# A tuned attention-and-MLP kernel: 11 of 29 products on zeros taken out, and all steps put in another order

## The chip, the cores and the metric

The kernel runs on one core of a Trainium2 chip. The metric is the device time of one execution in microseconds, the median of several. A profile of one further execution comes with it.

A core has five engines that run side by side, each with its own queue of instructions taken in order: PE (TensorE, matrix products; weight loads are shown as PEld), DVE (VectorE), ACT (ScalarE), POOL (GpSimd) and SP (SyncE, which issues most DMAs here). [...] An engine whose next instruction waits holds up all that stands behind it.

## The reference

Routed attention in 4 batches of 8 heads, 768 positions, 64 columns; each position is assigned to one of 16 centroids, and a query sees only keys of its own centroid. Then a gated MLP over all 3072 rows.

```python
q_assign = np.argmax(np.einsum('bhsd,hcd->bhsc', q_n, c_n), axis=-1)
k_assign = np.argmax(np.einsum('bhsd,hcd->bhsc', k_n, c_n), axis=-1)
mask = q_assign[:, :, :, None] == k_assign[:, :, None, :]
scores = np.where(mask, scale * np.matmul(q, k.transpose(0, 1, 3, 2)), -1000000000.0)
attn = np.exp(scores - max); attn = attn / (sum(attn) + 1e-09)
x = np.matmul(attn, v)          # heads side by side: 3072 x 512
h = x @ w_in                    # 512 x 2048
out = (h * (1.0 / (1.0 + np.exp(-h)))) @ w_out
```

## The kernel before

**Work.** Positions come in 6 tiles of 128 for keys (numbered 0 to 5) and 6 for queries (6 to 11). Heads are taken in pairs, 0 to 3. For each pair q and k are loaded into `nat`, turned so that the 64 columns lie along partitions, and put into `ab` in float16, together with a one-hot code of the centroid below them (rows 64 to 95). A product of 96 rows (L795, `scores`) then gives score and mask at once. ACT takes the exponential from a PSUM bank `M` into `P` (L798, 512 columns each). PE multiplies `P` by the values `vt` (L823, `pv`), DVE divides (L842 reciprocal, L847 product), PE or a DMA turns the result (L880) into `xt`, and `mlp` follows: up-products (L911), tanh on ACT (L921), gate on DVE (L924), down-products (L941), a copy out of PSUM (L187 on ACT, L189 on DVE) and a store.

**How the one-hot codes come about.** The first 8 tiles of each pair of the first batch are treated in one of two ways. Pairs 0 and 1 (`part4`): PE turns float32 (L611, 4 products of 128 columns for one head), ACT or DVE copies them to SBUF (`ev`, into `ot`), PE multiplies them in float32 by the centroids `st32` (L638, the program's 4 products a head, 8 records in the trace); DVE takes the maximum (L443), subtracts it (L446), marks the largest (L453); the scaled float16 copy (`hi`, L622 or L626) and the marks are turned on PE (L657, 8 products a head) and copied into `ab` (1024 columns, "s16"). Pairs 2 and 3 (`part2`): PE turns float32 (L689), ACT or DVE takes a high part straight into `ab` ("hip", L704 or L706), DVE a low part (L709), PE multiplies in float16 (L734 to L736), DVE marks and turns (L460, 32x32 blocks), and four copies put the codes into `ab` ("put"). The other 4 query tiles and the later batches (`part`) split into high and low (L482, L485), turn by a DMA on SP (L543) and multiply on PE (L558); their sums are made by DVE (L421).

**What sets the order.** No order of work stands in the loops. `build` makes a list of 1883 steps with what each comes after; the compressed list `PLAN` gives each buffer a slot, then the order of the steps, with the engine of each that has a choice. The last loop of the kernel unpacks it and issues the steps one by one, so each engine's queue is the plan's order restricted to that engine. A negative number in the plan is no step: it issues so many products on `zeros` (L1061, 128x256) into a bank that is free then; nothing reads them. A step's name is written here as batch.pair.head.first tile: for a0.1.0 (attention) batch.head.first query tile.

**The steps that the prediction follows.** Centroids: "cturn" turns them in float32 (L333) for `st32`, "cturn2" in float16 (L337, 2 products); "cp" are the copies into place, "cplace" three copies (L344 to L346). "lo" of p0.0.0.8 and p0.1.0.8 are the low parts of the four later query tiles of pairs 0 and 1, each followed by its transposition on SP.

Of the kernel before, what the change touches and what calls it, by code (L numbers as in the profile page):

```python
# [25 lines left out]
    "nl*;ZinTM2%>eCo(6r*rH4*cCch|zkgYh;i+&y*Q%k@LL9aXF)n5PGgXENwdh6IzH?n=^(Z$jp-Nj7i7=B~*m@--`Hb~XA;?SG2h1K)q%E9C80$m"
    "Zbv9SwSZcf8u+_jWXvXSlQc-hM^As0esb>b{-d%kQwA>qd0QL`KN$WSniK+6Z;bJ2@s6-CWbvVY4Q87nGawaI$@$fXSLfo8j_Yobf==_$JAF%V^Z"
    "4+be=L23;R3=L0rx-Dky_b-8(xW;_`(@0Vm(>AqK@&75@m+*A{#s!o2hmT3J-w-qwMM40<8(O#2eycV!K=QDN5-MNr?-w1c|n|#!c#+$o3wvq&lm"
    "qK3E4w#kQ&(6^QWu2Q}0XxI>NUZf#z^l;#JJ;vc0>@T-zxNc!&T)MfGHdgjx)Nhgmn2)+9h=2L<6$?_^%h|h*#R$>0{G*81<-!Dl|E=PI%NEzTve"
    "2$dS{W(>~X|i6|(mU+m(c@-(6pYO!ZK11dYetHAhS&rP=Bh@_ZO$o)a;(QSYnz@77Saa;2Im(VMtAtyQF%isLi8pYHiET6Gd_{6|cNM{8%u?tr^r"  # L30
    "0lTw~jeIx1+{)v(70YjWqHh$mtB%+cCwl7pyxodslzabZb&Ys_k5=mFemgezL*A^Qy<^a>A>!TDeM;C~8}KT~{RnitC%WEn*X{S#8uD_^t?>c-)R"
    "6ZraR2lPc&AA8%Od2>57?22y(Z}O`@K^-`d#AxPYj3cb<yu6$HbA(Tc^*<VfRe}|M|+f?+?G{gJ{Nut?#367_fN|`A>BW|KC~Y^XgQ{`!4d^v(s<"
    "Cb)5fvJB93fhV7l*cMaP6L}MVD?P0r4$6I@}Cj0E_qu*KjR}Gq5Px|f5G;`v*tJT}xyBF_NM{7WS8(}e~qBu@XuDW|KWU?mC)IE1qstU@<+xPrV1"
    "9UvpGPTfgCYTI!oQ9^l`<zT@8}3s8ZDgM3cN(J)KxU{7b)YW10u!MLw1%wE6k0$_s0VGK8N3LyU^dh@x#>7BLp$gKKfp`$w@16eCMXDVU=q9!Tj5"
    "7|6}G`-m;zHF2W*GU@Ca;y9?%n7K?iscvcWXy1iPRc&zz2a05hQ@?1mk1_g=s`fX-mfK6EF%1}oqWerd=C9mLK8zd?5Sl)ldLIhp~P;X~aU%>+%M"
    "h~5?Lh5in6<ulri;3Mph<!|iI<vX-H`UNb6hoCpiQ(Q3C9MT{U?UnK|b{}*<?14|<C#{kGoakXV0*z@mfw!=S!+cl($DuFugItOU=6s5N1}WHopl"
    "`s>unJzsH~rCpCcXkrSLO_%FE{!K45fdB{D%D~{e!W8fdSaVv?p2@6ogzbioUm@5IjsfE98gAX^)06a1<87SQrGwp#XD^X|K_jAsyc28QIY6@(=v"
    "U_<0yf{{{2}oP|Sr9^)6$%a9Mggp+U%u0meM-{ZQ%=sSvUbR2pL7MpkXIja@t^#6sv3*W*LxCVbKUl^MUx3P1>8dwYK6i>=;#Rf#6HQciW{a0iuT"
    "+!MTBjAT1<bWQqm$B~@JJ=6FdkDe9^gW8^MgN73@D+TcnnHgESkFU>(*7E~gkFcD^q*D^z;e|X+W(--lvCI~ID>sd`G~ziH3%&RYoHB04P~Jtlz}"
    "+-o_QtF$Ixfcw$KhLKs?-}zp(s|{Uki0I))a9Z=n=a(jLH5Pz&b4E#_50KY^+g&`;6%umCE;3(yU!F;+tRgIz;y-H*P-XeX$xXE0u!zRH>-h0n07"  # L40
    "Llx}iP!oG0e1Ri6qm!V7p2JvOXaQAew?vnq&#7)Im-X&YkN(n%YgoiRTG1|s|Hsg-3xi;=VoY^Hv8QXG3)E-slgd5pa;l9|`C2)Fmeg6moXPT^>I"
    "nB=@AErTuzSmAj6I9y=8$<9O6we;JrVNJ9*;I;PHlKj`^b0$>>=7`<s);ZqSIgiJP!rvdj$HZjxo0ml;^q6t2U_a(e8`xU>)_9kIa1&ZAO1%Xn;K"
    "oro)4b4b}eY9T|HOHma7OFF|j3OSOS{A1Kdh=futnOI1hE;q*0uVK9Tfe&}%3MsyH-g*^iO8eIm@@~ju2JAM6B7tv=p2M445VI=HSeL{P{2<-l_T"
    "(Pb5hi7JkH<W*9U*>#+y#jh-w}m%gwdxbP3O}sG9;tgOFI1<vZkP6(@q*ZepdI!P^t}zE72B#K^t}xOU=w|tVT*Et_Tyah1XN^RCDly&-i57-Z*;"
    "fLC+#H+gtE-t##&lqw}I`9&qRMj55OK6Lwg+jtT;r+!$IuwIy10;;`++UXYRE`xdOkaZoyGv;1=3|vD@fa#%3u#Xzx|5YtLvO!#=J$Kn~2NJpt-5"
    "))3lb*GGS6`~uIKtr(_Vg}E1%bJ(9V=L?tv`*>zm`no8F(M!yEReKH{V6Dz%bU)fvF#z|tW+M6;{H8qPx(@C~vh#;(7+MN=yfcY8zbbEF4rA}r{!"
    "r&B?WWKbPS8FHr&LE(D^<_vFAQ^;|0g%Ptoo-th9Xc77AiN<D~w%*^Eyx9n$A!9Yrsd$X@o99i^`ACSbl<Ys=?@UkN|(f$IN>borgY!R)a+F!&&A"
    "hp#jasUZ;G<?#A5e=qG3poq~qYFf@ZNY5#-IieoRvehj_AJH3bwgHP!zsXC#&L%&l_q4QOL(f#l=jDQ1h4Guyl=nSVh;38;CXa&=_E{?vM*y(%>$"
    "6%Moei@RX3|wbDDd=?OegHQWPqgD<0=xqKpg*L-O6Ckz9fDX$)4kyg+=L8xNy_skDz~9Ebcg290){{vSjD|=p|8oOs)LXP4(WWBswTi{<{d_tD@W"
    "yL_*S(7U53s_7eFP*tek-(a8%bYz7(AWmEjxOv$ZFzZwC4m41yK(_e3|M)6u~YVa{Xn8_ZPQgkvxndco_kMs-em4Wr;VJOG&#SFjy+z@Lf>xWl_m"  # L50
    ")>(^v9xmvex&MQ35j!h-m_5lya2+8wzGv<v`rn8AjD3NYMBhUPz)9r|LHRbi8Ad|^#uuUk;Rn@1olmeud955!EW#M*t#^RGh>cC?*UDWu#Xaw!W8"
    "q)83u~40$}{=h{%QIz@AEG9IPEWO9|YhX+M852(5u|LDSdZ!cA--ho2mnfMcN;tAv6{)s}`g6VKX0Nub`jNw-4g58$diHz+C0E@)A1<7OSQy#;`v"
    "|*Q>Uw=D|9hiS%#4-U=OQuRx!qFBM*bZqOCF!&C5+;vIg}IYoPw>b~j*c6P`C8x_B3L-=0#zz5<w<sj{cAPC>_EI;}x{Ki-lv@Yb-m}<206?-RI5"
    "A6jVpa<lFp0HZyoZ=o*X!nLjkeBD}rf-kliFPtP0<EDF41x9du`gN?<}vSQ#V&Rm#S#3XZyK}@6of)B6#7ADs03Z0E%b-N@D>b*Y1%&+0J)(Zw1="
    "@U5T?U;D55>$59>kbC`iN}jE;a$;Z1lOrof}xTX-7s@CSSz-tn-$OK4Yy`A`(fz;)I>Qhs1wX~+j<X+HyxW0ympg(t9&aF3%9kDUOCFjf1&9|gHs"
    "&k3Dla2c+^RXC~dM&`Yvm_VO~Q}iXFv+0`y`LPSYBe0FJWHbe4GPa%e4)|SXCtTMV05{-y5@icog?TT?M_f}CEk^$=^qkH-c$Bs6kuv^~-W{!``S"
    "hRH_a^hVq94=uGrA1@5gm<IXU-TjE7$x=-(HwU`xA|6?`daaY`Nkc`+&ZwX}?Q5llGMB_vyP7y99^YIK?UL;>_74<=G|JpN`BstuqZx!=EJ>-%b0"
    "BzTdd!FZ3Fmg$u9&zNP=3>NvUw9^gI~_06RG;`$nB26~XbLpmF|cP;ATCHat=a#K01bu#B+#_~Wq+@e1(I)SmT;27=WFcCW+{rO=A?LQ#14soup!"
    "?Tw#J_%}Kmtsx^d`){PWM<9>=q4yl|KIvXR*iz&*rgP2^uLczhBb;g+BM)8?6vSK+)&M-ueNfHdp@App`8oOgcd>zQ8cokw{<R{ceGB%3PLLF!iq"
    "KKJV5)7@)6BJUm83FIpIsyVzdJLvl2TCa~7+H!2;E2+W%4)?sD&P*mc;m&*)F*nsw;ss!hrr#y*4G^mjs!)At<uIr!ywSg-q`U#Q;EzfkoJ{SiF@"  # L60
    "&9UFmyP#QN1NKSS0$X91&RMR%sCue83O_(e`l`TB*t=nea**qv;obkh{#&uA8lYN0|4r3g#(dcI;HdJ7>(8T?v~TS7Kw{X>*f!-RWK&Io3##Xg&B"
    "gu*s&d_L$~El0XervyW0ygHr(Iroq1b{7*ymJV6?-}pb=E0{xnCvvDy!B(S$tfU>;Gh|1?@BFS@;L4FjkfM#bCc`A>;4B4dn=o#y+6B=KkdFoKk("
    "{UCYr9$-nS8eGxPn4q~6y{xKe=eOSI=ehl^y7z%H~FgT)mj!uDU%&)Gxh<#ZxfWE650<jQeEDjwD<29dkUtwNL#U^XtpuB@kupa8eRpmci)85kl0"
    "aCc`dG7TI_NNdJBVi*P(m9WAhG{Tec?IPaV~Q_m2#sJqEYLf^YY<}2IP^W342_|QVgW|+%nFPz;{L5@uYi^CG0cOPAwfB-Tt_RSH5LEp4CN2J0y|"
    "*|6o*~Vl>1IZU&6nW(AE&<nh&8H_8jF4b{n)A%+;834y_Brxo)QR7b=B)PIv7eEK)2oJ_6mXGXOe6clx%VvtTx?l@ICLs`|)UdSKU64WQiv)<I8*"
# [1032 lines left out]
```

## Time and profile before

| | us |
|---|---|
| three runs | 300.21, 300.11, 300.46 |
| median | 300.21 |
| the profiled execution, whole | 299.89 |
| the profiled execution, span from first to last instruction | 298.1 |
| its last product's end, from the start of the span | 294.97 |
| products on zeros | 29 |

The profiled execution is 1.8 us longer than its span, and 0.32 us shorter than the median. Times in the profile are counted from the span's start. A PE product's record lasts longer than the time until the next can begin, because products are pipelined: how fast they follow each other is read from the chain (the view that goes back from the last instruction to what released it, which gives each piece only the time that it adds), not from their durations.

### The profile page before, as it was taken

To read this page: it belongs to the slowest core of one execution; us is meant where nothing else is said; L and a number is where in the kernel's file an instruction comes from. 1 tells how busy PE (TensorE), PEld (TensorE's weight loads), DVE (VectorE), ACT (ScalarE), POOL (GpSimd) and SP (SyncE) were. 2 spreads that over 40 slices of the span, in tenths; PEclk is the share of its full clock that TensorE was granted. 3 is DMA by queue.
4 is the path that set the end of the run, shared out by engine and by line. 5 is a ranking of instruction groups with operands and counts; after the bars stand their busy time and mean duration, and the time that the engine had idled before them with its cause. 6 is when DMAs were issued, how large, how long until landed. Compare 5 with 4: busy or idle time off the path is not lost.

```text
span 298.1 us, 7899 instructions
## 1 busy us (share of the span) xinstructions
...
## 2 busy tenths in 40 slices
...
GB/s 221 209 304 239 247 264 294 298 231 208 270 248 196 286 256 204 114 213 228 225 158 104 104 244 153 131 93 31 28 26 70 30 3 62 35 109 0 2 50 161
DMA packets 81798, 47.32 MB, mean 159 GB/s; under 512 B 59104, under 2 KB 76768, under 8 KB 81760
## 3 DMA queue, kind: packets, MB, share of 16 engines
...
q14 instruction: 14, 0.11, 0.1%
q10 hardware_dynamic: 144, 0.03, 0.1%
...
## 4 chain that ended last, share of the span: by engine, by line
PE 93%; DVE 3%; POOL 1%; DMA 1%; issue 0%; SPq 0%
PE M L911 28%; PE M L941 28%; PE M L795 19%; PE M L823 11%; PE M L558 2%; PE M L638 1%; PE M L611 1%; DMA nat<-in_k_dram 1%; PE M L1061 1%; PE M L657 1%; PE M L880 1%; POOL vt L189 0%; DVE lo L709 0%; POOL hl L482 0%; DVE hl L485 0%
## 5 line engine op out<-in xcount | busy, mean ns | idle before, releaser
L798 ACT ACTIVATE P<-M 128x512 f16<-128x512 f32 x288 | 153.5, 633 | 12.9 <-PE M L795 12.5
L924 DVE SCALAR_TENSOR_TENSOR gq<-tn,M 128x384 f16<-128x384 f32 (+1 forms) x120 | 65.7, 574 | 49.1 <-ACT tn L921 47.0
L911 PE MATMUL M<-xt,win_s 128*128 128x384 f16 (+1 forms) x576 | 95.9, 308 | 0.0
L941 PE MATMUL M<-wout_s,gq 128*128 128x512 f16 (+1 forms) x400 | 93.3, 370 | 0.0
L795 PE MATMUL M<-ab 96*128 96x256 f16 (+1 forms) x432 | 89.5, 307 | 0.3 <-DVE M L421 0.2
L921 ACT ACTIVATE tn<-M 128x384 f32<-128x384 f32 (+1 forms) x120 | 59.6, 522 | 28.0 <-PE M L911 25.1
L911 PEld LDWEIGHTS <-win_s 128*128 128x128 f16 x576 | 55.0, 97 | 29.4
L189 POOL COPY ab<-ohT 32x384 f16<-32x384 f16 (+2 forms) x65 | 35.2, 543 | 99.0 <-PE M L795 34.7
L941 PEld LDWEIGHTS <-gq 128*128 128x128 f16 x400 | 37.2, 97 | 35.5
L823 PEld LDWEIGHTS <-P 128*128 128x128 f16 x1152 | 45.7, 97 | 9.7 <-issue 0.4
L823 PE MATMUL M<-vt,P 128*128 128x65 f16 x1152 | 49.0, 193 | 0.2 <-DVE oh L453 0.2
L795 PEld LDWEIGHTS <-ab 96*128 96x128 f16 x432 | 37.8, 97 | 17.5 <-issue 1.4
L187 ACT COPY ot<-M 128x512 f32<-128x512 f32 (+1 forms) x18 | 10.4, 583 | 22.0 <-PE M L941 18.1
L485 DVE SCALAR_TENSOR_TENSOR hl<-nat,hl 128x768 f16<-128x768 f32 (+1 forms) x28 | 26.1, 931 | 0.2
L421 DVE TENSOR_REDUCE M<-M 128x192 f32<-128x384 f32 (+1 forms) x28 | 15.2, 544 | 8.5 <-PE M L558 4.8
L460 DVE STREAM_TRANSPOSE ohT<-oh 128x384 f16<-128x384 f16 (+2 forms) x30 | 16.9, 563 | 1.5 <-ACT ab L187 0.7
L189 POOL CAST vt<-nv 128x384 f16<-128x384 f32 x20 | 12.5, 639 | 18.9 <-DMA nv<-in_v_dram 18.5
L189 DVE COPY ot<-M 128x512 f32<-128x512 f32 (+1 forms) x11 | 7.0, 647 | 10.7 <-PE M L941 10.7
L482 POOL TENSOR_SCALAR hl<-nat 128x768 f16<-128x768 f32 (+1 forms) x16 | 12.4, 778 | 5.3 <-DMA nat<-in_q_dram 3.2
L853 DVE TENSOR_TENSOR xn<-M,rz 128x384 f16<-128x384 f32 x24 | 13.2, 553 | 0.7
L558 PEld LDWEIGHTS <-ab 128*128 128x128 f16 x320 | 11.8, 96 | 2.7 <-issue 0.2
L443 DVE TENSOR_REDUCE mx<-M 128x12 f32<-128x192 f32 (+2 forms) x33 | 11.4, 346 | 2.2 <-PE M L638 1.6
...
## 6 DMA issues: line engine op xcount, KB each, us to landing
...
```

The costliest lines, as they stand in the source:

```text
L189: eng(en).tensor_copy(out, in_)
L421: e.nc.vector.tensor_reduce(out=bank(dst)[:, at : at + HC * n].rearrange("p (n c) -> p n c", c=HC), in_=bank(src)[:, 0 : 32 * n].rearrange ...
L460: e.nc.vector.transpose(T(ohT)[:, 0:n, :].rearrange("p n c -> p (n c)"), T(oh)[:, 0:n, :].rearrange("p n c -> p (n c)"))
L485: e.nc.vector.scalar_tensor_tensor(out=dl(), in0=src(), scalar=QS, in1=dh(), op0=ALU.mult, op1=ALU.subtract)
L558: e.nc.tensor.matmul(bank(Lb)[:, 32 * i : 32 * i + 32], a, st, start=True, stop=True)
L795: e.nc.tensor.matmul(bank(sb)[:, at : at + 128 * (c - a)], ab[0:96, kt[m], :], q, start=True, stop=True)
L798: e.nc.scalar.activation(out=T(P)[:, 0:n], in_=bank(sb)[:, 0:n], func=AF.Exp, bias=0.0, scale=ESC)
L823: e.nc.tensor.matmul(bank(O)[:, at : at + D + 1], T(P)[:, c : c + 128], T(vb)[:, VW * m : VW * m + D + 1], start=(m == 0), stop=(m == NJ - ...
L911: e.nc.tensor.matmul(bank(bk)[:, c0 : c0 + n], e.win_s[:, r, ts(fb, 128)], T(X)[:, r, 128 * j0 : 128 * j1], start=(r == 0), stop=(r == NR ...
L921: e.nc.scalar.activation(out=T(tn)[:, 0 : n * per], in_=bank(bk)[:, 0 : n * per], func=AF.Tanh, bias=0.0, scale=1.0)
L924: e.nc.vector.scalar_tensor_tensor(out=gq(f0 // 4)[:, f0 % 4 : f0 % 4 + per, 0:n], in0=T(tn)[:, 0 : n * per].rearrange("p (f c) -> p f c", ...
L941: e.nc.tensor.matmul(bank(bk)[:, 0 : c1 - c0], gq(quarter)[:, fc % 4, ts(t, 128)], e.wout_s[:, fc, c0:c1], start=(fc == 0), stop=(fc == NF ...
```

## The change

Only `PLAN` is another one. No function changes, and the same 1883 steps are done on the same data.

```diff
 PLAN = (
-    "c-mE&2mDXf8^`Z=|Mn&sAuA&zv`A%U?^#A!nOWIHGD6A7%1S9JLXi<d8D&?LO?GyY7613=-1EKqd%fO$o-^*f=RW6oo^yZSe2(7<IF949D$BKfPR"
...
+    "c-mc=2mFrJ`^WERe;2;Xj%05kWM=QZDY9oO5~4_m%<SyFS11W7D<dgnL`HU*MfUi;Kj%KrQ~!Ux-hHk!?sK2}oa?&I`9Ap^zvFQn@H#%nF_vq4oP"
...
 )
```

Unpacked, the two plans differ in three ways.

- **Products on zeros.** Before: 11, then 5, 2, 2, 3, 2, 3 and 1 (29 in all). After: 11, then 1, 1, 2, 1 and 2 (18).
- **Engines.** 118 steps have another engine. Among the early ones: the copy of a value tile pair (cast of `vt`, cv0.0, first head) from POOL to ACT; the high part of p0.1.0.8 from POOL to DVE; one "hip" of pair 3 from ACT to DVE; the float16 copies (`hi`) of p0.0.0.0 and p0.1.1.0 from ACT to POOL, that of p0.1.0.0 from POOL to ACT; the weights' cast cin1 no longer among DVE's first 60 steps. By counts over the program: ACT 461 to 467 steps, POOL 122 to 119, SP 149 to 146, DVE 461 in both.
- **Order.** Nearly every engine's order. The beginnings, one line a step, PE left before and right after ("zeros 5" are five products on zeros):

```
PE before                     PE after
zeros 11                      zeros 11
turn f32 p0.0.0.0  (L611)     turn f32 p0.0.0.0
zeros 5                       zeros 1
cturn2  (L337)                cturn   (L333)
cturn   (L333)                turn f32 p0.0.1.0
zeros 2                       zeros 1
turn f32 p0.0.1.0             cturn2
centroids p0.0.0.0 (L638)     centroids p0.0.0.0
zeros 2                       centroids p0.0.1.0
centroids p0.0.1.0            turn f32 p0.1.1.0
turn f32 p0.1.1.0             turn f32 p0.1.0.0
turn f32 p0.1.0.0             turn codes p0.0.0.0
turn codes p0.0.0.0 (L657)    centroids p0.1.1.0
centroids p0.1.1.0            centroids p0.1.0.0
turn codes p0.0.1.0           scores a0.0.0 (two banks)
centroids p0.1.0.0            centroids p0.0.0.8 (L558)
turn f32 p0.2.0.0  (L689)     turn codes p0.0.1.0
scores a0.0.0                 zeros 2
centroids p0.0.0.8 (L558)     turn f32 p0.2.0.0
scores a0.0.0                 turn codes p0.1.1.0 (both heads)
scores a0.1.0                 scores a0.1.0
scores a0.0.0                 turn f32 p0.2.1.0
turn f32 p0.2.1.0             scores a0.1.0
turn codes p0.1.1.0 (both)    centroids p0.1.0.8 (L558)
scores a0.1.0 (two banks)     scores a0.3.0
zeros 3                       scores a0.1.0
```

```
DVE after, from its 7th step: cp2.0, lo p0.0.0.8, max p0.0.0.0, cp1.2, below, mark p0.0.0.0,
  clear, max p0.0.1.0, below, cplace, hi p0.1.0.8, lo p0.1.0.8, mark p0.0.1.0, max p0.1.1.0,
  below, sum p0.0.0.8, mark p0.1.1.0, max p0.0.0.8
DVE before, from its 8th:     cp2.1, lo p0.0.0.8, max p0.0.0.0, below, mark, max p0.0.1.0, below,
  mark, lo p0.1.0.8, cplace, max p0.1.1.0, below, sum p0.0.0.8, mark p0.1.1.0, max p0.0.0.8
ACT after:  ev p0.0.0.0, ev p0.0.1.0, cp2.1, hi p0.1.0.0, cp0.2, ev p0.1.1.0, cast cv0.0,
  ev p0.1.0.0, s16 p0.0.0.0, exp, s16 p0.0.1.0, hip p0.2.0.0, exp, exp, hip p0.2.1.0, exp, exp
ACT before: ev p0.0.0.0, hi p0.0.0.0, cp2.0, cp0.2, ev p0.0.1.0, cp1.2, hi p0.1.1.0, ev p0.1.1.0,
  ev p0.1.0.0, s16 p0.0.0.0, s16 p0.0.1.0, hip p0.2.0.0, exp, exp, exp, exp, hip p0.2.1.0, exp
SP after, loads by pair: q0, k0 head 0, k0 head 1, later q0, k1, q1, v0, later q1, q2,
  turn p0.0.0.8, k2, q3, later q2, turn p0.1.0.8
SP before:  q0, k0 head 0, later q0, k0 head 1, k1, q1, later q1, q2, k2,
  turn p0.0.0.8, v0, later q3, turn p0.1.0.8
```

From the middle of the first batch on, the same steps stand in both plans a few places apart; the first up-product (L911) is PE's step 111 before and 112 after, and the last nine steps are down-products of the last unit in both.

More of the change, by code (lines that the diff above doesn't have):

```diff
@@ L26 @@
[L26 to L65, printed above, removed]
@@ new lines @@
+    "ZOg>~}(_*OdK~eW=&8gs{ET1)T6dvb?5m5d3B=cg&EfcSj2M@fh1N@6}s8#_~k!9Q&+edwcBLJdxUf9l`HJ@w{W&f(E~xo6q+4I0@$Mj+4U7GT@{"
+    "%UlMd;%$EeQebjj=`^?-^VW+@OHtl*>$ce{}u`8xA5~xo!v-Qy5?<CoE(wD|z#nP5+>k?^CFe~e>LA?1!w-m6e>Bo+<^VK|)%{;wk<$Y%MnxDH4@"
+    "%%S|nkX|9wTF0LkpH@)Mf2Y{vo`LU=*_9@*bX&OXcDbKQ{(4-K~svh`{_0BcGo>%R>&PcVEZRgP6df(H#KgQ-SdFmM~_*DK*R_1Pqg(lzui;Eu7+"
+    "d1!Ds5jBf5L%ez#-%!(-;?voj3)K``PKUe+aGW)fq*-)H^}@ozFDnCC*~$)NdHGfZK2-pAZLc85Y{J)=xdeNU3@p&2AnmT$z;C(ihgV?8hIcgbd!"
+    "j`6NIGoz3hDT(@M^KPx4W7^!gYgb*r)mvhzNfG%v?Qbfx`#$4q$!2WF%re33SI~N=`noF<WB1Jcl7M+r(2f`49qt!+&Fn+wUwu_PePXFgio|UovI"
```

61 lines of the change are left out of this document (48 added, 13 removed).

## The prediction

> **What bounds the kernel now.** I read the page's chain first, then the windows, then the chain piece by piece.
>
> ```profile
> PE 93%; DVE 3%; POOL 1%; DMA 1%; issue 0%; SPq 0%
> ```
>
> The chain is PE for 93% of the span. What is not PE lies at one place, as the windows show (columns: stretch, length, then busy time of PE, PEld, DVE, ACT and POOL).
>
> ```profile
> 1.00:4.00 3.00, 2.72 (x12) 1.71 (x13) 1.73 (x9) 1.00 (x1) 1.28 (x5) 1.00 0.59 177
> 4.00:7.10 3.10, 3.10 (x15) 2.15 (x15) 0.99 (x5) 1.47 (x4) 1.49 (x13) 1.00 0.97 318
> 16.30:29.00 12.70, 12.00 (x182) 9.69 (x181) 12.20 (x29) 12.70 (x27) 9.62 (x19) 1.00 1.04 268
> 40.00:295.00 255.00, 254.97 (x2568) 162.88 (x2566) 177.58 (x399) 195.63 (x396) 52.36 (x78) 1.00 0.61 145
> ```
>
> From 40 us to 295 us PE is busy for 254.97 of 255.00 us: an order can win nothing there, it can only lose. From 16.3 to 29 us ACT has no pause and DVE hardly one; PE is the one that waits. So the change is decided before about 35 us. The chain in order of time (start, length, what) says the same:
>
> ```profile
> 1.24 2.44 DMA nat<-in_k_dram
> 3.68 0.14 issue
> 3.81 1.09 PE M L611 x4
> 4.90 1.07 PE M L1061 x5
> 5.97 0.35 PE M L337 x2
> 6.32 0.35 PE M L333
> 6.67 0.43 PE M L1061 x2
> 7.10 0.53 PE M L611 x4
> 7.63 0.81 PE M L638 x8
> 8.44 0.22 PE M L1061 x2
> 8.66 0.81 PE M L638 x8
> 9.47 0.91 PE M L611 x8
> ...
> 16.29 0.10 POOL ab L189
> ...
> 28.47 0.50 DVE oh L453 x2
> ```
>
> The chain starts with a load, is PE from 3.81 to 16.29 us, goes through POOL and DVE until 28.97, and from there on is PE to the end but for the last copy. Two things are to be seen. First, five products on zeros cost 1.07 us (0.214 each) at 4.90, and two cost 0.22 (0.11 each) at 8.44: the same product at half and at full speed, with the step near 7.2 us (the four transposes cost 1.09 us at 3.81, eight 0.91 at 9.47). The page's granted clock reads full in all these windows, so the halving is read from these rows. Second, 1.07 + 0.43 + 0.22 = 1.72 us of zeros stand on the chain before 16 us.
>
> **The change, part by part.** *Zeros before the first scores.* 5 + 2 + 2 become 1 + 1. At the rows' prices 1.72 us go and 2 x 0.214 = 0.43 stay: 1.29 us, if PE found all its inputs ready. It won't. The work that moves forward also runs longer at half speed, and the second head's transposes now need their load sooner. PE after, by those rows: transposes until 4.90; one zero, 5.11; the centroids' float32 turn, 0.35, 5.46 (its DVE input is ready, below); the second head's four transposes at half speed, 4 x 0.214 = 0.86. Their load moves one place forward on SP; it can land anywhere from 4.7 us (the 2.44 us of the row at 1.24, plus an issue) to 6.0 us (where the load ahead of it landed before, POOL's row below); I take 5.5 us, nearest to the landings around it. So 6.4 us; one zero, 6.6; cturn2 0.35, 7.0; the first head's centroid products 0.81, 7.8, partly before the clock's step; the second head's, 8.6, against 8.66 + 0.81 = 9.47. **PE is about 0.85 us ahead at 9.5 us**, 0.4 to 1.2 by the landing's two ends.
>
> *What DVE makes of it.* What follows needs DVE's marks. DVE rows of before, with one of POOL:
>
> ```profile
> 4.47 0.25 DVE L321 TENSOR_SCALAR cn<-tn,ci 128x64 f32<-128x64 f32 x1
> 7.52 0.69 DVE L485 SCALAR_TENSOR_TENSOR hl<-nat,hl 128x512 f16<-128x512 f32 x1
> 8.48 0.29 DVE L443 TENSOR_REDUCE mx<-M 128x8 f32<-128x128 f32 x1 [0.26 <-PE M L638]
> 8.80 0.30 DVE L446 TENSOR_TENSOR M<-M,mx 128x128 f32<-128x128 f32 x1
> 9.13 0.35 DVE L453 TENSOR_SCALAR gq<-M 128x96 f16<-128x96 f32 x2
> 13.06 0.42 DVE L443 TENSOR_REDUCE mx<-M 128x16 f32<-128x256 f32 x1 [1.33 <-PE M L638]
> 13.52 0.43 DVE L446 TENSOR_TENSOR M<-M,mx 128x256 f32<-128x256 f32 x1
> 14.02 0.43 DVE L421 TENSOR_REDUCE M<-M 128x128 f32<-128x256 f32 x1
> 14.36 0.48 DVE L453 TENSOR_SCALAR gq<-M 128x192 f16<-128x192 f32 x2
> 6.03 0.62 POOL L482 TENSOR_SCALAR hl<-nat 128x512 f16<-128x512 f32 x1 [1.61 <-DMA nat<-in_q_dram]
> ```
>
> Before, DVE idled 1.33 us ahead of 13.06, waiting for pair 1's centroid products. After, it has no such pause, but more to do first. The later queries' load goes back one place on SP (one issue, 0.47), so POOL's high part is done at 6.5 + 0.62 = 7.1, DVE's low part at 7.9, and the first maximum begins at about 7.95 instead of 8.48. Then, in the new order and with 0.03 between instructions (less an overlap like that from 14.02 to 14.36, 0.09, ahead of some): maximum 0.32, cp1.2 0.42, subtraction 0.33, marks 0.36, a clear 0.15 (no dearer than the copy of 0.21 at 11.04), maximum 0.33, subtraction 0.33, cplace 0.72, high part of p0.1.0.8, low part 0.62, marks 0.38, maximum 0.45, subtraction 0.47, sum 0.35. (cp1.2 took 0.42 us on ACT; cplace is three copies, the first of them the row at 11.04, with gaps of 0.03.)
>
> ```profile
> 8.15 0.42 ACT L187 COPY st<-M 64x64 f16<-64x64 f16 x2
> 11.04 0.21 DVE L344 COPY stk<-M 64x128 f16<-64x128 f16 x1
> 24.00 0.69 DVE L706 TENSOR_SCALAR ab<-M 128x512 f16<-128x512 f32 x1
> 25.93 0.94 DVE L189 CAST win_s<-gq 128x1024 f16<-128x1024 f32 x1
> ```
>
> The high part is not seen on DVE from SBUF: the same shape from PSUM took 0.69, half of the 1024-column cast is 0.47; I take 0.6. The sum is 5.83 us, so pair 1's marks begin at 13.78 instead of 14.36: **0.58 us earlier**. The rest of PE's 0.85 is lost to DVE's longer row.
>
> *From there to the end of DVE's stretch.* DVE is full (12.20 of 12.70), so its load counts. In comes one "hip", 0.69; out goes cin1, 0.94, to a later time, and the windows show DVE with room after 40 us (177.58 of 255). One put leaves and one comes. That is 0.25 us less, and 0.58 + 0.25 = **0.83 us** in all, if ACT follows. If cin1 should cost its 0.94 all the same, the "hip" alone stands against the 0.58, and nothing is won (the second rival).
>
> *Zeros after the first scores.* 3 + 2 + 3 + 1 become 2 + 1 + 2. I cost that at nothing:
>
> ```profile
> 16.33 0.49 PE L1061 MATMUL M<-zeros 128*128 128x256 f16 x3
> ```
>
> The first of them stand where the chain has left PE (from 16.29), so what hides them is a wait; with the wait gone they would cost 0.11 each, 4 fewer giving 0.44.
>
> *ACT.* Its rows:
>
> ```profile
> 13.53 0.60 ACT L704 ACTIVATE ab<-M 128x512 f16<-128x512 f32 x1 [0.33 <-PE M L689]
> 14.03 2.06 ACT L798 ACTIVATE P<-M 128x512 f16<-128x512 f32 x4
> ```
>
> Exponentials follow each other every 0.49 us: four in 2.06, of which the last is some 0.60 by itself, (2.06 - 0.60) / 3. After, the first can begin near 12.3 (the first head's codes are turned on PE from 9.5, right behind DVE's marks; ACT is free for their copy at 10.7, behind two copies for pair 1 and the cast; then come two banks of scores), but with the second s16 behind it, which waits for marks at 12.5 on DVE and then eight turns on PE: 13.2. From there ACT has no pause but one near 15 us, where it waits 0.3 for pair 1's scores behind DVE's marks. The cast that comes to ACT costs about 0.5 between two copies before 10.7. One "hip" less gives 0.49 back later. These cancel to within 0.3 us, so ACT by itself is even; that DVE's 0.83 shows in the end rests on DVE being the one that the chain passes through, not ACT.
>
> **Sum:** 299.89 - 0.83 = 299.06 for an execution like the profiled one; the median of the runs lies 0.32 above it: **299.4 us**. Its own range, by the landing's ends and 0.3 for ACT, is 298.9 to 299.8.
>
> **The rivals.**
>
> *All waits shrink.* The plan puts zeros where a pause is expected, and it has fewer. If the nine zeros' places in the first 31 us close up (0.44) and the 16.3 to 29 us stretch loses its PE idle time (12.70 - 12.00 = 0.70, modelled ends making this a lower count), 0.44 + 0.70 come on top: 299.4 - 1.1 = 298.3. Against it: ACT is full in that stretch and its exponentials are the same number.
>
> *The exponentials keep the pace.* ACT is busy 12.70 of 12.70 us. If it, not DVE, holds PE, only its own row counts, and that is even: 300.2.
>
> *The clock's step comes later.* With seven fewer zeros PE idles near 5.5 us, in the stretch that before was full (3.10 of 3.10) just ahead of the step. If the step then slips, the two heads' centroid products and the eight transposes (0.81 + 0.81 + 0.91 = 2.53 us) can take up to twice as long; pair 1's maximum on DVE waits for all of them, less the 0.85 us that PE had gained, 1.7 us: 299.4 + 1.7 = 301.1. It decides if PE's busy share there falls to that of the first 4 us, 2.72 of 3.00 busy by modelled ends, which did not bring the step. For it: the change takes away just what kept PE busy. Against: PE still has transposes and turns there. [...]
>
> *A transposition on SP starves the exponentials: slower.* PE's 25th step is now the centroid product of p0.1.0.8, before three of the scores that ACT wants next. It needs that tile's DMA transposition.
>
> ```profile
> 11.15 1.24 SPq L543 DMA_TRANSPOSE ab<-hl  x1
> ab<-hl SPq DMA_TRANSPOSE x28, 5.1
> ```
>
> DVE's low part ends at about 12.1 now (7.95 plus the terms up to it, 4.19), so the issue is 1 us later than 11.15, and the median landing is 5.1 us after issue: 17.2, while PE reaches that step at about 16. ACT would then lose some 1.2 us; one "hip" less offsets 0.49: 300.2 + 0.7 = 300.9. It decides if it lands after about 16.5. Before, PE asked for it only after 18 us.
>
> **How the numbers follow.** Forecast 0.40; all waits shrink 0.16; the exponentials' pace 0.18; late step 0.12; starved 0.14. A measurement of this kernel can tell about 0.2%, 0.6 us: faster means below 299.6. Of the forecast's own range 0.28 lies below it and 0.12 above; with 0.16 that is 0.44 faster. Within: 0.12 + 0.18 = 0.30. Slower: 0.12 + 0.14 = 0.26. The range reaches from 298.2 to 301.3.
>
> **What would show it.** The chain after should have L638 twice in a row, ending near 8.6; DVE's L453 of 192 columns at 13.8; no pause of DVE ahead of L443 near 13; the first 512-column exponential near 12.3. A granted pair of zeros that still takes 0.21 after 7.2 us would show the late step; an ACT pause near 17 us behind L558 the starving. PE idle after 40 us would make all of this wrong, since nothing here counts on it.

## The result, and the profile after

| | before | after |
|---|---|---|
| median of four runs, us | 300.16 (300.04 to 300.46) | 303.45 (302.73 to 303.72) |
| ratio | | 1.0104 (95% interval 1.0085 to 1.0123) |
| the profiled execution, whole, us | 299.89 | 302.73 |
| its span, us | 298.1 | 300.9 |

The change made the kernel 3.3 us slower; 299.4 had been forecast, at most 301.3. Some executions here are slower as a whole: of the 75 of the kernel before beside the experiments, nine took 307.65 to 308.39 us and the others 299.19 to 302.45; here and below ratios leave such ones out, and medians don't. First the page's chain of the changed kernel:

```profile
PE 82%; DVE 6%; DMA 3%; ACT 2%; issue 2%; POOL 2%; SPq 1%; DVEq 0%; ACTq 0%; POOLq 0%
```

It was PE for 93%. The windows of the changed kernel (stretch, length, busy time of PE, PEld, DVE, ACT, POOL, then clock and DMA) say where PE was lost:

```profile
4.00:7.10 3.10, 3.10 (x17) 2.41 (x16) 1.12 (x6) 1.42 (x4) 0.47 (x1) 1.00 0.79 249
16.30:29.00 12.70, 11.81 (x171) 9.20 (x169) 11.81 (x32) 12.06 (x26) 8.78 (x17) 1.00 1.18 256
30.00:40.00 10.00, 8.98 (x154) 7.45 (x152) 9.41 (x28) 9.63 (x21) 6.92 (x11) 1.00 0.88 247
40.00:295.00 255.00, 254.17 (x2569) 162.67 (x2568) 174.89 (x397) 198.20 (x402) 51.84 (x80) 1.00 0.60 143
13.50:41.00 27.50, 25.57 (x405) 20.87 (x404) 25.80 (x72) 26.49 (x53) 17.89 (x31) 1.00 1.05 256
```

Two stretches of before that were not shown yet:

```profile
30.00:40.00 10.00, 10.00 (x181) 8.61 (x178) 8.93 (x33) 10.00 (x21) 9.19 (x16) 1.00 0.89 257
13.50:41.00 27.50, 26.78 (x432) 22.64 (x431) 25.64 (x73) 27.47 (x57) 21.02 (x38) 1.00 0.99 251
```

Three things are to be seen. From 30 to 40 us PE is busy 8.98 us instead of 10.00. From 40 to 295 us it has 254.17 where it had 254.97: 0.8 us are lost where, before, nothing was. And ACT, which had no pause from 13.5 to 41 us (27.47 of 27.50), now stands still for 1.0 us there.

The same from the starts of the products: what passes from one start to the next beyond the price of the product at full clock (0.109 us for 256 columns, of which one record lasts 0.27, and so on), zeros counted as lost, adds up as follows. PE is ahead by 0.4 us until 30 us, and then loses three times.

| lost by PE, us, up to | 15 us | 30 us | 40 us | 45 us | the end |
|---|---|---|---|---|---|
| before | 5.89 | 9.00 | 9.91 | 10.00 | 10.38 |
| after | 5.41 | 8.56 | 11.08 | 11.68 | 13.00 |

The early steps came as forecast, or sooner. From the timelines of PE, DVE and ACT of the changed kernel:

```profile
6.70 2.00 PE L638 MATMUL M<-st,ot 128*128 128x32 f32 x16
13.16 0.48 DVE L453 TENSOR_SCALAR gq<-M 128x192 f16<-128x192 f32 x2
12.47 0.60 ACT L798 ACTIVATE P<-M 128x512 f16<-128x512 f32 x1 [0.71 <-PE M L795]
13.14 1.01 ACT L187 COPY ab<-M 96x1024 f16<-96x1024 f16 x1
14.04 0.60 ACT L704 ACTIVATE ab<-M 128x512 f16<-128x512 f32 x1
14.53 1.08 ACT L798 ACTIVATE P<-M 128x512 f16<-128x512 f32 x2
```

The two heads' centroid products end at 8.70, and pair 1's marks begin at 13.16, 1.2 us earlier than before. But look at ACT: the first exponential at 12.47 only changed places with a copy and a "hip"; the unbroken row begins at 14.53, where before it began at 14.03. The eighth exponential starts at 17.96 us, against 17.85. Then ACT runs dry, as its timeline after and then before shows:

```profile
16.96 2.09 ACT L798 ACTIVATE P<-M 128x512 f16<-128x512 f32 x4
19.69 1.61 ACT L798 ACTIVATE P<-M 128x512 f16<-128x512 f32 x3 [0.64 <-PE M L795]
```

```profile
16.89 3.61 ACT L798 ACTIVATE P<-M 128x512 f16<-128x512 f32 x7
```

Why it does stands in the chain of the changed kernel:

```profile
13.74 5.10 DMA nat<-in_k_dram
18.84 0.04 issue
18.89 0.55 PE M L689 x3
19.43 0.24 PE M L795 x2
19.69 4.06 ACT P L798 x8
...
31.93 0.87 DVE vt L189
...
34.39 0.30 DVE oh L453
34.69 0.04 issue
34.74 0.82 PE M L795 x6
...
42.40 0.81 DVE hl L485
43.21 0.55 issue
43.76 0.56 DVE M L421
44.33 0.04 issue
44.37 0.60 PE M L911 x4
...
148.07 1.38 DVE hl L485
149.45 0.48 DVE gq L924
149.97 0.81 PE M L911 x4
...
193.73 3.15 DMA ab<-ohT
...
197.01 0.58 DVE ohT L460
197.58 0.03 issue
197.62 0.25 DVE ab L189
197.87 0.03 issue
197.90 0.56 DVE gq L924
198.46 0.04 issue
198.50 0.81 PE M L911 x4
```

Read from above: PE's float32 turn of p0.3.1.0 (L689) waits until the last load of k lands at 18.84, with the scores that ACT wants behind it. At 34 us a PSUM bank is held until DVE has made the marks of p0.3.0.8, behind a cast of 0.87 us that has come from POOL. At 44.37 and 149.97 an up-product waits for a bank that DVE frees late, behind a long low part (L485). At 198.5 it waits for a gate, queued behind a transposition of codes (L460) that waits for a copy by DMA. And the first up-product starts at 41.89 us where it started at 39.83, since the last exponential of the first query tiles, which it needs from all eight heads, starts at 38.10 instead of 35.54.

### The profile page after: what moved, and what is told of

It reads as the page before. It is cut to its first block, busy times and chain, and to the rows that moved or that the text cites. A ratio compares the mean times of both kernels' runs of the same rounds, so it can differ in the third digit from the quotient of the medians.

```text
span 300.9 us, 7860 instructions
## 1 busy us (share of the span) xinstructions
PE 293.5 (98%) x3069; PEld 194.5 (65%) x3069; DVE 208.9 (69%) x502; ACT 232.5 (77%) x469; POOL 74.4 (25%) x135
## 4 chain that ended last, share of the span: by engine, by line
PE 82%; DVE 6%; DMA 3%; ACT 2%; issue 2%; POOL 2%; SPq 1%; DVEq 0%; ACTq 0%; POOLq 0%
PE M L941 27%; PE M L911 25%; PE M L795 18%; PE M L823 10%; PE M L558 2%; DMA nat<-in_k_dram 2%; ACT P L798 2%; DVE hl L485 1%; POOL ab L189 1%; DMA ab<-ohT 1%; DVE gq L924 1%; DVE ab L189 1%; DMA tn<-in_centroids_dram 1%; SPq L410 1%; DVE ohT L460 1%
## 5 line engine op out<-in xcount | busy, mean ns | idle before, releaser
L798 ACT ACTIVATE P<-M 128x512 f16<-128x512 f32 x288 | 151.9, 629 | 15.3 <-PE M L795 13.4
L911 PE MATMUL M<-xt,win_s 128*128 128x384 f16 (+1 forms) x576 | 94.6, 308 | 0.8 <-DVE gq L924 0.6
L941 PE MATMUL M<-wout_s,gq 128*128 128x512 f16 (+2 forms) x400 | 93.7, 370 | 0.0
L911 PEld LDWEIGHTS <-win_s 128*128 128x128 f16 x576 | 55.4, 97 | 30.4 <-issue 1.6
L189 POOL COPY ab<-ohT 32x384 f16<-32x384 f16 (+2 forms) x62 | 33.8, 545 | 70.7 <-DVE ohT L460 25.0
L795 PEld LDWEIGHTS <-ab 96*128 96x128 f16 x432 | 38.1, 97 | 18.8 <-issue 3.9
L187 ACT COPY ot<-M 128x512 f32<-128x512 f32 (+2 forms) x21 | 11.9, 571 | 22.0 <-PE M L941 18.3
L485 DVE SCALAR_TENSOR_TENSOR hl<-nat,hl 128x768 f16<-128x768 f32 (+1 forms) x28 | 27.4, 985 | 2.0 <-POOL hl L482 1.5
L482 POOL TENSOR_SCALAR hl<-nat 128x768 f16<-128x768 f32 (+1 forms) x20 | 16.3, 818 | 25.2 <-DMA nat<-in_k_dram 12.7
L460 DVE STREAM_TRANSPOSE ohT<-oh 128x384 f16<-128x384 f16 (+2 forms) x30 | 16.7, 560 | 6.6 <-DMA ab<-ohT 5.7
L189 POOL CAST vt<-nv 128x384 f16<-128x384 f32 x17 | 8.7, 514 | 29.5 <-DMA nv<-in_v_dram 29.0
L842 DVE RECIPROCAL rz<-M 128x6 f32<-128x6 f32 (+1 forms) x36 | 6.5, 182 | 13.5 <-PE M L823 13.0
L558 PEld LDWEIGHTS <-ab 128*128 128x128 f16 x320 | 11.5, 96 | 3.0 <-DMA ab<-hl 0.3
L453 DVE TENSOR_SCALAR oh<-M 128x96 f16<-128x96 f32 (+3 forms) x56 | 12.1, 255 | 0.7
```

The costliest lines, as they stand in the source:

```text
L189: eng(en).tensor_copy(out, in_)
L460: e.nc.vector.transpose(T(ohT)[:, 0:n, :].rearrange("p n c -> p (n c)"), T(oh)[:, 0:n, :].rearrange("p n c -> p (n c)"))
L482: e.nc.gpsimd.tensor_scalar(out=dh(), in0=src(), scalar1=QS, scalar2=1.0, op0=ALU.mult, op1=ALU.mult)
L485: e.nc.vector.scalar_tensor_tensor(out=dl(), in0=src(), scalar=QS, in1=dh(), op0=ALU.mult, op1=ALU.subtract)
L558: e.nc.tensor.matmul(bank(Lb)[:, 32 * i : 32 * i + 32], a, st, start=True, stop=True)
L795: e.nc.tensor.matmul(bank(sb)[:, at : at + 128 * (c - a)], ab[0:96, kt[m], :], q, start=True, stop=True)
```

## The experiments

All are timed beside the kernel before on the same chip, whose medians were 300.2 to 300.5 us. Diffs show the unpacked plan.

### The zeros alone, and the zeros put back

e1_before_few_zeros is the kernel before, with the changed kernel's zeros at the start:

```diff
-PE: turn p0.0.0.0, zeros 5, cturn2, cturn, zeros 2, turn p0.0.1.0, centroids, zeros 2, centroids
+PE: turn p0.0.0.0, zeros 1, cturn2, cturn, zeros 1, turn p0.0.1.0, centroids, centroids
```

> The kernel before, with the early products on zeros as in the change: 5 become 1, the first 2 become 1, the second 2 go; nothing else differs. If the new order of the steps made the loss (A), this stays within 0.5 us of before: 299.7 to 300.3 us, since DVE and ACT pace the stretch from 16 to 29 us. If the removed zeros made it (B: the clock's step slips), L638 runs slower at 7 to 8 us and the time rises by 1 to 3 us, to 301.2 or more. If each zero on the chain had counted (C), 1.29 us go: 298.9 us.

Ratio 1.0036 (1.0004 to 1.0069), some 1.1 us slower: outside A's range, far from C, and at the lower end of B's. But B's late step is not in its profile, where it comes at 6.99 us (7.16 before). PE has lost 9.04 us by 30 us there, as before (9.00): taking out zeros won nothing, since what PE gains at first it waits off again by 15 us, for loads (0.7 us ahead of its float32 turns, 0.2 before) and for DVE. This profile loses its time later, 1.2 us in three pauses at 52 to 77 us, two of them behind casts of weights on DVE that had waited for their loads. Whether the missing zeros have a part in that is not shown. The runs in the ratio spread from 299.6 to 303.1 us, and three of them had a mean granted clock of 0.993, which none of the 75 runs of the kernel before beside these experiments had (0.998 at least).

e13_after_zeros_back is the reverse, and e12_after_again is the changed kernel once more, to compare with:

```diff
-PE: turn p0.0.0.0, zeros 1, cturn, turn p0.0.1.0, zeros 1, cturn2
+PE: turn p0.0.0.0, zeros 5, cturn, turn p0.0.1.0, zeros 2, cturn2
```

> The changed kernel with the zeros of before at its start: five products on zeros instead of one behind the first float32 turn, two instead of one behind the second. Nothing else. Theory A (the zeros hold the clock): the profile shows the clock's step at 4.4 to 7.8 us, no run of this kernel has a mean granted clock under 0.997, and all runs lie within 1 us of each other, the median at 302.3 to 302.9; the unmended order of the steps still costs its 2.5 us. Theory B (the zeros do nothing; late steps and falls back come by chance): the runs spread as those of the changed kernel did, 302.1 to 304.8.

> The changed kernel as it is, profiled a second time and timed beside the others. Theory A: its first profile was a lucky one, since the transposition of p0.1.0.8 landed at 15.6 us there and at 16.3 to 17.0 in the six kernels made from it; here L558 of that tile begins at 16.3 or later, behind a pause of PE, and the eighth exponential at 18.6 or later (17.96 in the first profile). Theory B: the early moves of the other kernels made it late; here it is 15.6 and 18.0 again.

e12: 302.83 us, 1.0096 (1.0062 to 1.0129), with L558 at 15.59 and the eighth exponential at 17.98, so the first profile was no single lucky one. But e2, e4 and e7 below have the same steps in the same order up to 30 us, and there the transposition of p0.1.0.8 took 4.4 to 5.0 us from issue to landing, where it had taken 3.7. PE waited 0.5 to 1.1 us for it, and the eighth exponential started at 18.65 to 19.30. When this DMA lands differs from one execution to the next. L558 in the timelines of the changed kernel and then of e2:

```profile
15.62 0.36 PE L558 MATMUL M<-stk,ab 128*128 128x32 f16 x8
17.01 0.36 PE L558 MATMUL M<-stk,ab 128*128 128x32 f16 x8 [1.08 <-DMA ab<-hl]
```

e13: 303.93 us, 1.0102 (1.0068 to 1.0136), a microsecond above what its theory A had. With the zeros back the changed kernel is no faster: in e13's profile PE has lost 6.43 us by 15 us, 1.0 more than in the changed kernel, so its lead is gone. The missing zeros, then, are not what the changed kernel lost its time by. With the new order they are what its early lead is made of; on the kernel before, taking them out won nothing (e1).

### One loss at a time

e2_after_puts_pool takes the copies of codes off SP:

```diff
-two copies of the codes of p3.2.0.0: SP
+two copies of the codes of p3.2.0.0: POOL
```

> The changed kernel, with two of the four copies of the codes of p3.2.0.0 (the last two) on POOL instead of on SP. In the changed kernel they landed at 196.7 and 196.9 us, and DVE's next L460 waited 5.7 us for them, with gates queued behind it; PE then lost 0.47 us at 198. If that wait made that loss (A), this is 0.4 to 0.5 us faster than the changed kernel, 303.0 us, and PE has no gap at 198. If PE would have been held there anyway by ACT (B), the time stays at 303.4.

302.71 us, 1.0081 (1.006 to 1.0101). DVE's wait for the copy, 5.7 us in the changed kernel, is 2.6, and PE's pause at 198 us (0.47 us, and 0.25 in e12) is gone.

e7_after_pool_apart moves two steps on POOL's queue and nothing else:

```diff
-POOL: cin0, cout3, high p1.1.0.0, cin5, put, cin2 ... high p3.1.0.0, high p3.2.0.0, put
+POOL: cin0, high p1.1.0.0, cin5, put, cin2, cout3 ... high p3.1.0.0, put, high p3.2.0.0
```

> The changed kernel with two steps moved on POOL alone: the cast cout3 (41.89 us, 1.14) goes behind cin2, to 50.4 us, and the high part of p3.2.0.0 (147.81 us, 0.83) behind the put at 154.28. Neither is needed before 67 and 167 us. DVE's queue is not touched. Theory A: DVE's low parts (L485, 128x768) took 1.52 us at 42.32 and 1.46 us at 147.99 instead of 0.95 because POOL worked on SBUF beside them; with POOL idle they take 0.95, and PE's two pauses of 0.44 us at 43.83 and 0.40 us at 149.5 go: 0.8 us in all. Theory B: DVE's length there is its own or another engine's doing: they stay at 1.4 or more, and so do the pauses.

302.75 us, 1.0083 (1.0067 to 1.01). DVE's timeline of the changed kernel has the first two rows, that of e7 the next two:

```profile
42.32 1.52 DVE L485 SCALAR_TENSOR_TENSOR hl<-nat,hl 128x768 f16<-128x768 f32 x1
147.99 1.46 DVE L485 SCALAR_TENSOR_TENSOR hl<-nat,hl 128x768 f16<-128x768 f32 x1
```

```profile
42.90 0.95 DVE L485 SCALAR_TENSOR_TENSOR hl<-nat,hl 128x768 f16<-128x768 f32 x1
148.32 0.95 DVE L485 SCALAR_TENSOR_TENSOR hl<-nat,hl 128x768 f16<-128x768 f32 x1
```

Both are 0.95 with POOL idle, and the windows of e7 have PE busy without a break where both pauses were:

```profile
42.00:45.00 3.00, 3.00 (x55) 2.71 (x52) 2.97 (x8) 3.00 (x7) 0.00 (x0) 1.00 0.98 303
147.00:151.00 4.00, 4.00 (x37) 2.53 (x35) 4.00 (x8) 3.70 (x9) 0.00 (x0) 1.00 0.40 126
```

Shown: POOL's work beside them cost these two low parts 0.5 us each, and PE 0.84 us. How much it costs depends on how they happen to fall together: in e12, the changed kernel once more, the second low part takes 1.13 us, and PE's pause at 150 us isn't there. For e2 and e7 it is the traces that tell; their times can't be told from e12's.

e4_after_cast_pool:

```diff
-cast of cv0.2: DVE (0.87 us, ahead of the marks of p0.3.0.8)
+cast of cv0.2: POOL
```

> The changed kernel, with one cast of values (cv0.2, first head) back from DVE to POOL, as before the change. It took DVE 0.87 us at 31.9, ahead of marks whose bank two scores of a0.7.0 waited for: PE lost 0.66 us at 34.0 and ACT paused 0.5 at 34.7. If DVE's long items made that (A), 0.3 to 0.6 us faster than the changed kernel, 303.0 us. If the exponentials were late anyway (B), 303.4, and the gap only moves.

304.38 us, 1.0114 (1.0082 to 1.0146). In its profile PE loses 1.76 us from 30 to 35 us instead of 2.31, so the cast is at most a part of that loss. Whether it is worth time stays open: the runs fall in two groups, two of 302.2 and 302.4 us, the profiled one among them, and four of 304.4 to 304.6, of which no profile was taken.

e3_after_k3_early:

```diff
-SP: ... later q2, turn p0.1.0.8, later q3, last load of k
+SP: ... last load of k, later q2, turn p0.1.0.8, later q3
```

> The changed kernel, with the load of pair 3's keys moved on SP from behind the second transposition to ahead of a load of queries that comes before it. PE waited 0.64 us for this load at 18.2 us, and ACT paused 0.64 us at 19. If the exponentials' pace sets the first 40 us (A), the pause shows in full: 0.5 to 0.8 us faster, 302.7 us, and one more exponential done at 20 us. If DVE's row sets it (B), nothing: 303.4.

303.11 us, 1.0091 (1.0065 to 1.0116). The load lands at 14.9 us instead of 18.8, but the transposition of p0.1.0.8 behind it at 16.6 instead of 15.6, and PE waits for that one: the eighth exponential starts at 18.93. One DMA wait stands in place of the other. It need not be the move that brought it, since that transposition landed as late in e2, e4 and e7 without it. So this run doesn't decide between A and B.

### Mends of the order from 16 to 40 us

e5_after_round0_first and e15_mended_round0 move exponentials of the first eight query tiles forward, in two ways; e8_after_four_mended is e5's move with three mends more; e10_after_later_asks moves the two PE steps that ask for DMAs back:

```diff
 e5, e8
-ACT: a0.2.4, a0.5.0, a0.3.4, a0.0.4, a0.1.4, a0.5.0, a0.0.4, a0.7.0 x3, a0.3.4, a0.6.0 x3
+ACT: a0.5.0, a0.0.4, a0.1.4, a0.5.0, a0.0.4, a0.7.0 x3, a0.6.0 x3, a0.2.4, a0.3.4, a0.3.4
 e10
-PE: centroids p0.1.0.8, five scores ... turn p0.3.1.0, score a0.1.4, centroids p0.2.1.0, score a0.3.0
+PE: five scores, centroids p0.1.0.8 ... score a0.1.4, centroids p0.2.1.0, score a0.3.0, turn p0.3.1.0
 e15, against e14
-ACT: a0.3.4, a0.0.4, a0.1.4, a0.5.0, a0.0.4, a0.7.0 x3, a0.3.4, a0.6.0 x3
+ACT: a0.3.4, a0.0.4, a0.5.0, a0.7.0 x3, a0.6.0 x3, a0.1.4, a0.0.4, a0.3.4
```

> The changed kernel with one move: the scores and exponentials of a0.2.4 and a0.3.4 that stand ahead of a0.7.0 and a0.6.0 on PE and ACT (three of each) go behind the last exponential of a0.6.0. Theory A: up-products need the first query tiles of all eight heads, and the last of these exponentials, a0.6.0, starts at 38.1 us after but 35.5 before; with three exponentials of 0.48 us out of its way it starts near 36.7, the first up-product L911 comes near 40.5 instead of 41.89, PE's idle time from 30 to 35 us (2.3 us beyond full rate) falls to about 1.0, and the time falls by 1.0 to 1.5 us, to about 302. Theory B: PE there only keeps ACT's pace, one score for each bank that an exponential frees, whichever head it is of: the idle time stays at 2.0 or more, and the time changes by less than 0.4 us.

> The changed kernel with four mends at once: the codes' copies of p3.2.0.0 on POOL instead of SP, the cast of cv0.2 on POOL instead of DVE, the two POOL steps apart from DVE's low parts, and the exponentials of a0.2.4 and a0.3.4 behind a0.6.0. Theory A (the changed kernel loses its 3.3 us at these four places, and its start is some 0.5 us ahead): the places give 0.47 + 0.5 + 0.8 + 1.2 = 3.0 us, so about 300.0 to 300.5, level with the kernel before. Theory B (the loss is spread, or mended places only hand their wait on to the next): 301.5 or more.

> The changed kernel with two PE steps asking later for what a DMA brings: the centroid product of p0.1.0.8 (L558, waits for the DMA transposition) behind five scores instead of ahead of them, and the float32 turn of p0.3.1.0 (L689, waits for the last load of k) behind three more steps; its copy on DVE goes one step back too. No engine of any step changes. Theory A (ACT sets the pace from 14 to 40 us, and it runs dry behind these two DMAs): ACT's 16th exponential begins near 22.0 us instead of 22.6 in the profile of the changed kernel and 22.8 to 23.4 in the runs made from it, its idle time from 13.5 to 41 us falls from 1.0 or more to 0.4 or less, and the time falls by 0.6 to 1.0 us, to about 302.5. Theory B (ACT's row is not what holds the end, DVE's is): the exponentials come earlier, but banks are freed no sooner, the 40th exponential stays at 34.2 or later, and the time changes by less than 0.3 us.

> e14 and the exponentials of a0.7.0 and a0.6.0 three places earlier on ACT, ahead of one of a0.1.4 and one of a0.0.4, with their scores earlier on PE, and the pv and division of a0.0.4 and a0.1.4 behind those of a0.6.0 and a0.7.0. Unlike the earlier try, the early scores of a0.2.4 and a0.3.4 stay as a stock for ACT. Theory A (what is left is that up-products need all eight heads, and two exponentials more stand ahead of the last of them): the last of the first eight heads' exponentials comes 0.9 us earlier against the 46th exponential than in e14, the first up-product too, and the time falls by 0.5 to 1.0 us, level with before or under it. Theory B (PSUM banks, held by what waits for DVE, set the pace of the scores): the scores moved ahead only wait for a bank, ACT runs dry as in e5, and the time is the same or longer.

| | time, us | ratio and interval |
|---|---|---|
| e5 | 305.01 | 1.0171 (1.0152 to 1.019) |
| e8 | 307.75 | 1.0245 (1.0215 to 1.0275) |
| e10 | 305.20 | 1.0142 (1.0103 to 1.0181) |
| e15 | 306.49 | 1.0185 (1.0147 to 1.0223) |

None is faster than the changed kernel, so theory A fails in each as it was put; e5, e8 and e15 are slower, and e10's interval overlaps that of e12 beside it. In e5 the time of theory B, hardly a change, fails too. e5, e8 and e15 also have a few tiles on other PSUM banks than the kernels that they come from (2, 1 and 24 of 557), as the new orders need. e5 shows how the time went, in the window of its 13.5 to 41 us:

```profile
13.50:41.00 27.50, 23.14 (x364) 18.82 (x362) 24.32 (x67) 25.20 (x49) 17.43 (x31) 1.00 1.05 259
```

ACT works 25.20 us, 1.3 less than in the changed kernel. The scores of a0.2.4 and a0.3.4 had lain ready in banks since 26.3 and 27.4 us; that stock may have fed ACT while full banks kept new scores out. e15 left the stock in place and lost all the same: ACT stands still for 2.2 us up to 41 us, against 1.0 in e14, and the first up-product comes at 44.60 us. That fits theory B of e15, that the banks set what PE can do for ACT here; but PE's longest pause in both (0.9 and 1.0 us, near 39 us) ends with an exponential, not with DVE, so which banks it was is not shown. e8's profile has half clock from 39.97 to 46.79 us, and e10's has its clock step only at 13.08, so neither serves for its own question.

### All mends together

e11_after_mended has the two PE steps of e10, the mends of e2, e4 and e7, and the exponentials in the changed kernel's order; e14_mended_zeros_back has the zeros of e13 too.

> The changed kernel with all mends that a trace has borne out, and the order of the exponentials left as it is: the two PE steps asking later, the cast of cv0.2 and the codes' copies of p3.2.0.0 on POOL, and the two POOL steps apart from DVE's low parts. Theory A (the loss lies at these places): 0.7 + 0.5 + 0.47 + 0.84 = 2.5 us off the changed kernel, so about 301.0. Theory B (what is left is the later first up-product, 41.89 us instead of 39.83, which none of these mends by more than 1 us): it is 301.5 to 302.0, with the first up-product after 41 us and PE's lost time still 1 us above before at 45 us.

> The kernel with all mends that a trace bore out (e11) and the zeros of before at its start. e11 ran at 300.4 to 301.7 us in five of its twelve runs, three had a mean granted clock of 0.994 (302.2 to 302.9), and in its profile the clock stepped up at 22.78 us. Theory A (both the zeros and the order cost): no run under 0.997, step at 4.4 to 7.8 us, median 300.5 to 301.2; what is left above before, 0.5 to 1 us, is the later first up-product. Theory B (zeros do nothing): the spread of e11 again, median 302 or more.

e11: 302.49 us, 1.0065 (1.0036 to 1.0094); its profiled execution took 308.73 us, with the clock's step at 22.78, and isn't read here. e14: 301.94 us, 1.005 (1.0024 to 1.0076), between its two theories. e13 and e14 ran on one chip and differ by the mends alone: 303.93 against 301.94, so the mended places are worth 2.0 us by the medians and 1.6 by the ratios, whose intervals just overlap (priced at 2.5). What is left is about 1.5 us: e14's first up-product comes at 42.15 us, and it has lost 11.45 us by 45 us where before has lost 10.00.

### One suspected cause given to the kernel before

Mending the changed order often moved something else too. These two dose the kernel before instead. Their orders need other PSUM banks for some tiles (14 of 557 in e16, 19 in e17), so a dose is not quite alone.

```diff
 e16_before_late_up
-PE, ACT, DVE: first eight up-products with their tanh and gate, from 39.83 us
+the same 16 steps 2.06 us later in each queue
 e17_before_early_asks
-PE: seven scores, centroids p0.1.0.8, twelve more steps, turn p0.3.1.0
+PE: centroids p0.1.0.8, seven scores, turn p0.3.1.0, twelve more steps
```

> The kernel before with one dose of what the changed order has: the first eight up-products (L911) with their tanh and gate stand 2.06 us later in the queues of PE, ACT and DVE, as far as the first up-product comes later after the change (41.89 against 39.83 us). Nothing else is moved. Theory A (with no up-products PE has only scores, one for each bank that ACT frees, so that work in reach is what PE lacks at 30 to 45 us): PE loses 0.8 to 1.2 us more between 39 and 45 us, and the time is 0.8 to 1.2 us above before, about 301.2. Theory B (the scores and pv that now stand ahead fill the place, and a later first up-product by itself costs nothing): the time is within 0.3 us of before.

> The kernel before with the two PE steps that wait for DMAs standing as early as after the change: the centroid product of p0.1.0.8 (L558) ahead of six scores, the float32 turn of p0.3.1.0 (L689) at 18.4 us instead of 22.15. The DMAs themselves stay: the transposition landed at 16.2 us, the last load of k at 19.5. Theory A (ACT sets the pace from 14 to 40 us; a PE step that waits for a DMA holds back the scores behind it, and ACT runs dry): PE waits about 1.1 us ahead of that L689, ACT has a pause of 0.5 to 1.0 us near 19.5 us where before it had none, and the time rises by as much, to about 301. Theory B (PE catches up before ACT notices, or a later slack takes it): within 0.3 us of before.

e17: 301.78 us, 1.0052 (1.0032 to 1.0073). PE's timeline in e17, and the window of e17:

```profile
18.24 0.30 PE L689 MATMUL M<-ident,nat 128*128 128x128 f32 x1
19.20 0.55 PE L689 MATMUL M<-ident,nat 128*128 128x128 f32 x3 [0.66 <-DMA nat<-in_k_dram]
```

```profile
13.50:41.00 27.50, 25.11 (x411) 21.18 (x410) 24.45 (x70) 26.46 (x54) 20.23 (x37) 1.00 0.96 247
```

ACT stands still for 1.04 us, where before it had no pause, and the time rises by 1.5, more than theory A had: theory A in kind. The place is a little off: ACT's pauses lie at 21.1 us (0.39) and after, not at 19.5, for the two steps also hold their banks longer, and these runs can't tell one from the other.

e16: 302.93 us, 1.0091 (1.0072 to 1.0111). The window of e16 at the place of the dose:

```profile
38.00:42.00 4.00, 3.19 (x38) 2.54 (x36) 3.30 (x10) 4.00 (x9) 2.80 (x4) 1.00 0.96 312
49.00:56.00 7.00, 5.97 (x69) 4.56 (x67) 5.03 (x10) 5.91 (x13) 3.32 (x4) 1.00 1.14 294
87.00:89.00 2.00, 1.23 (x20) 0.79 (x19) 1.28 (x2) 2.00 (x5) 1.65 (x2) 1.00 0.93 298
```

PE stands still for 0.8 us between 38 and 42 us, as theory A has it (1.13 by the starts of its products: 0.41 at 38.9 and 0.71 at 40.0), while ACT goes on without a pause. That is not all: PE loses another 1.0 us between 49 and 56 and 0.8 us at 87 to 89, so this dose costs 2.7 us, more than the 2.06 it moved and far more than theory A had, and nothing of it was won back later. The loss at 87 to 89 is a wait for a DMA transposition that SP issued at 82.11 us instead of 79.45.

e9_hybrid16 puts the other half to the test: the changed kernel's steps, engines and zeros up to 16 us (100 steps), then the order and the engines of before, with other banks for 18 tiles. Expected before it ran were 299.5 to 299.8 us if the early lead keeps its worth and all of the loss lies in the later order, 300.2 if DVE's and ACT's full row swallows the lead, and above 301 if the changed start itself brings what is lost later. It took 301.71 us, 1.006 (1.0032 to 1.0087). In its profile the later queries' load lands later, and POOL's high part starts at 7.15 us (6.63 in the changed kernel); the eighth exponential starts at 18.68, and PE has lost 1.2 us more than before by 30 us. Its first up-product comes at 41.34 us. So the changed start, ahead of the order of before, costs time too, and the loss doesn't lie in the later order alone. Whether the start costs it by itself, or only where the two halves meet, is not shown.

## Why the prediction was wrong

**PE ahead at the start: right.** 0.85 us was forecast by 9.5 us; the second head's centroid products end at 8.70 instead of 9.47, 0.77 earlier. Two sizes were off and cancelled: the second head's load was there by 5.15 us, not 5.5, and the 16 centroid products took some 0.2 us longer than 0.81 a head.

**DVE's marks: right, and better.** 13.16 us, forecast 13.78, before 14.36; DVE had no pause ahead of its maximum.

**0.83 us "in all, if ACT follows": the step that failed first.** The sum took 0.58 + 0.25 = 0.83 us from DVE's row and said that DVE is the one that the chain passes through. The row of before had both, DVE 12.20 and ACT 12.70 of 12.70 us, and what followed went with the fuller one. With the eighth exponential at 17.96 against 17.85, DVE's lead of 1.2 us brought the exponentials nothing; 0.4 us of it is seen on PE at 15 to 30 us and is gone by 35. The rival "the exponentials keep the pace" had this right, though not the time.

**A DMA that starves the exponentials: the rival had the mechanism, not the place.** It named the transposition of p0.1.0.8; in the changed kernel's profile that landed at 15.57, not 17.2, ahead of its deciding point of 16.5. But the next PE step of the kind, the turn of p0.3.1.0, waited for its load until 18.84, and ACT paused for 0.64 us; the forecast had not looked up when that load lands and where PE would ask for it. In e2 and e7, with the same steps up to there, it was the other way round: the transposition landed at 16.96 and 16.95 as the rival had it, and the load was there in time. On the kernel before, asking early for both cost 1.5 us (e17).

**"An order can win nothing there, it can only lose", said of 40 to 295 us, with the loss put at nothing: the step that failed most.** With it fell "the change is decided before about 35 us". 1.61 us more were lost from 30 to 40 us, 0.51 from 40 to 45, and 0.94 after, together 3.06 against a lead of 0.44. The prediction had named the sign itself: PE idle after 40 us. Of the 1.45 us after 40 in that profile, 0.84 are POOL beside DVE's low parts (e7) and 0.47 the codes' copies on SP (e2). Of the 1.61 before, the cast on DVE is 0.55 at most (e4). The rest goes to the later up-products and to the banks held for DVE; on the changed kernel these could not be told apart (e5 and e15 failed), and that stays open. That later up-products can cost as much is shown by e16, on the kernel before, with its change of banks. In its queue on PE the first up-product stands one step later than before, but ahead of the last exponential that it needs there are 46 others where there were 42, and the prediction didn't look there. That count alone doesn't explain its time: e5 and e15 brought it to 43 and were slower, and e9 has 42 and a first up-product at 41.34. Nor is all of the loss the later order's, as e9 shows.

**The zeros: half right.** At the start they are worth PE's lead, as the sum had it, but it lasts to 15 us only with the new order (e1 and e13), and it buys nothing at the end. The four later ones, priced at nothing, were not tried alone.

**The late clock step: did not happen in the changed kernel's profiles** (6.80 and 7.11 us). What the rival took to bring it, PE's idle time, did not come about either: PE was busy for 3.10 of 3.10 us from 4 to 7.1. In e10, whose first steps are the same, PE was busy for 2.90 us there, and the step came at 13.08. That idle time puts the step off was the author's assumption; one such profile doesn't show it.
